# Block-sparse attention and a max-out feed-forward on one core: weights' squares on TensorE, eight places for the weights' loads, queries of four units at once, single-column biases, early sampled copies on GpSimd

## The chip, the core and the metric

One core of one Trainium2 chip. The metric is the device time in microseconds (us) of one execution. Engines are named as in the profile: PE (TensorE; PEld is its weight load), DVE (VectorE), ACT (ScalarE), POOL (GpSimd), SP (SyncE, here a queue of DMA issues).

## What is computed

Four batches (B = 4) of eight heads (H = 8), 768 positions (S), head size 64 (D): attention in which each block of 32 queries sees its neighbours, the first and the last block, and three sampled blocks; the queries of the first and the last block see all keys. The 3072 rows of 512 that come out go through a max-out feed-forward.

```python
scores = q @ k.T / sqrt(64)          # kept where |blk_i - blk_j| <= 1, or either block is 0 or 23,
attn = softmax(scores)               # or blk_j is one of the 3 blocks sampled for blk_i
x = (attn @ v) as [3072, 512]
h = max(x @ w1, x @ w2, x @ w3)      # [512, 768] each
out = h @ w_out                      # [768, 512]
```

## The kernel before

**Numbers in pairs.** Each float32 operand is scaled by a power of two and split into a high and a low half-precision part (ACT writes the high part, DVE the low part, or POOL for some); a product is three matmuls (`PASSES`). The scale comes from a sum of squares: ACT's `Square` with an accumulator, then a one-column matmul against `ones` that adds over the partitions (`total`), then three small DVE operations (`scale_of`).

**Units.** A batch has 24 blocks: one global unit "G" (first and last block, against all keys) and eleven sparse units of two blocks. 48 units U run in the order G, the last pair, then the rest; x = U % 12 is the place in the batch. A sparse unit gathers its keys on chip into `kg` (sampled blocks by three copies per block, one each on DVE, POOL and ACT, L595; the window by DVE, L602) and its values by POOL's indirect DMA (L608). Then per half of the heads an item: scores on PE (L677) into one of two pairs of PSUM banks, row maxima on DVE (L656), the bias (maximum times minus the scale, L658), exponentials on ACT (L686), the probabilities turned: in units under `TURNED` by PE, ACT and DVE (L628 to L631), later by ACT's high part, POOL's low part and a DMA transpose on SP (L635, L636, L639), three places (`NPH`) for the parts. Then values on PE (L701), the division on DVE (L759 to L761), and a turn into `xg` (L768 to L773). Queries are prepared 128 rows at a time (`prep_q`, two units; twice the buffer `qn`).

**Feed-forward.** Every four units make 256 rows, and step F of twelve runs 18 groups of 12 matmuls (six f, three weights, L795): the first weight's result goes to `hf` by ACT (L799), the others by DVE's maximum (L802), then the high part to `ht` by ACT (L805) and the low by POOL (L806); three buffers `hf`. Then 36 matmuls with w_out (L819). `ht` has two buffers, F % 2.

**Weights.** Eight groups g (six of w1, w2, w3 and two of w_out), three tiles each: SP loads them as shifted 16-bit data (L364, L367) into one of four places (three in the key buffer `kt1` of the second batch, one in `xg2`), POOL casts a part into `ob` (L371), DVE joins the two (L375) into the float32 tile `m`, which lies in `ht[g % 2]`. ACT squares the whole group (L386), PE adds, DVE scales, ACT and DVE write the two parts (L398, L406). The groups of w_out are split last, when all scales are known (`relative`, L422 to L429).

**The order** on each engine is fixed before the launch by a planner (`Plan.order`): each operation has an assumed cost, the keys that it reads and writes, and a priority (a unit's number; for weights `WPRI + WSL * g`); a key that is rewritten waits for all its readers. Engines then run their lists in order.

Of the kernel before, what the change touches and what calls it, by code (L numbers as in the profile page):

```python
# [30 lines left out]
NK, NPR, NPH, NPT = 2, 3, 3, 4  # L31
PV, TURNED, POOL_LOW = 0.2, 4, ()
TP, HOLD, WPRI, WSL = 0.45, 3.0, 2.5, 0.25
# [111 lines left out]
def tile_block_sparse_attention_maxout_ffn(ctx, tc, q, k, v, sampled, w1, w2, w3, w_out, out):  # L145
    nc = tc.nc
    B, H, S, D = q.shape
    P = 128
# [37 lines left out]
    qn = sbuf([P, H, D], F32, "qn", 2)  # L186
    qt = sbuf([P, 2, G, P], F16, "qt", 2)
# [11 lines left out]
    ht = sbuf([P, NF, 2, 256], F16, "ht", 2)  # L199
# [110 lines left out]
    def registers(t, name, js, pri):  # L310
        def load():
            for i in js:
                block_of((V, L, A)[t], i, t)
        plan.add(name, 0.56 * len(js), load, r=["samp"], w=[("regs", t, js[0])], pri=pri)
# [24 lines left out]
    def next_stage():  # L339
# [3 lines left out]
    kt1 = kts[1].rearrange("p n t g e s -> p (n t g e s)").bitcast(F32)  # L343
    w_stage = [(kt1[:, 1024 * i : 1024 * i + 1024], [("kt", 1, i), ("kt", 1, 3 + i)]) for i in range(3)]
    w_stage += [(xg[i].rearrange("p g t x -> p (g t x)").bitcast(F32),
                 [(y, i, c0) for y in ("xh", "xl") for c0 in range(0, 256, 64)]) for i in (2,)]

    def decode_w(g, pri):

        c = g % 2  # L350
        m = ht[c].rearrange("p f t x -> p (f t x)").bitcast(F32).rearrange("p (k x) -> p k x", k=3)
        mi = m.bitcast(I32)
        mk = [("ht", c, f) for f in range(NF)]
        for k in range(3):
            st, stk = w_stage[(3 * g + k) % len(w_stage)]
# [36 lines left out]
    def split_w(g, parts, sc, keys, pri):  # L392
        m3, hi, lo, mk = parts
        for k in range(3):
            n = m3.shape[1] // 3
            sl = slice(k * n, (k + 1) * n)
            s, mkk = sc[k % len(sc)], mk[2 * k : 2 * k + 2]
# [7 lines left out]
            else:  # L405
                plan.add("DVE", 0.74, lambda sl=sl, s=s: V.scalar_tensor_tensor(  # L406
# [74 lines left out]
    def turn_k(b, pri):  # L481
        sm, sts, kt = ksm[b % 2], k_sts[b], kts[b % NK]
        for a in range(3):
            src = stage[sts[a]].rearrange("p (e g x) -> p e g x", e=2, g=G)
            for half in range(2):
# [8 lines left out]
                hk, lk = [("kt", b % NK, 3 * t + a) for t in range(2)]  # L494
                plan.add("PE", TP, turn, r=SK(sts[a]) + ["ident", ("k", "s", b)], free=[hk, lk],
# [38 lines left out]
    def prep_q(b, n, pri):  # L534
# [381 lines left out]
```

## Time and profile before

| what | value |
|---|---|
| device time, 3 runs | 694.62 us median (694.61 to 694.68) |
| the profiled execution: its own time, its span | 689.42 us, 687.5 us |
| busy PE, DVE, ACT, POOL | 591.3, 411.8, 392.1, 316.8 us |
| mean granted TensorE clock | 0.916 |

The span is counted from the first instruction to the last; the profiled execution's own time is 1.9 us longer than its span, and 5.2 us under the median of the plain runs. A share of busy time is a mean over stages: here a stage of loading and decoding weights, a long one, and a tail. Idle time of an engine matters only where it holds the end.

### The profile page before, as it was taken

The numbers are of one execution on the slowest core, as the hardware profiler recorded it, in microseconds if no ns is written. First come the engines' busy times: TensorE is split into PE (matmuls) and PEld (weight loads), VectorE is DVE, ScalarE is ACT, GpSimd is POOL, SyncE is SP. The second block draws the span as 40 slices with busy tenths as digits, with TensorE's granted clock in tenths as the row PEclk, the third lists the DMA queues.
The fourth block names the chain that finished last, engine by engine and source line by source line (L and its number), as shares of the span: only waits on it lengthen the run. The fifth ranks groups of instructions, "written<-read, shape, count | busy, mean of one in ns | idle before, by whom it ended". The sixth has DMA issues, their size and how long they took to land.

```text
span 687.5 us, 25107 instructions
## 1 busy us (share of the span) xinstructions
PE 591.3 (86%) x10576; PEld 442.2 (64%) x10576; DVE 411.8 (60%) x1022; ACT 392.1 (57%) x830; POOL 316.8 (46%) x414
## 2 busy tenths in 40 slices
PE   2586468359999979999999789989999789999997
PEld 2354347236885856875876666866776675778684
DVE  1678779983666876498555664676547675422110
ACT  4646667667636766776547656855558556312121
POOL 1354356463534665364554563446455756511110
PEclk9756559559999989999999999999999999999999
DMA  9684788779967799987997889996987979830000
GB/s 212 187 249 131 233 217 202 159 151 221 222 121 169 92 200 211 199 198 165 169 169 138 148 177 174 195 234 132 188 126 148 176 144 174 175 61 25 17 17 32
DMA packets 197044, 109.28 MB, mean 159 GB/s; under 512 B 161073, under 2 KB 182594, under 8 KB 196930
## 3 DMA queue, kind: packets, MB, share of 16 engines
q1 hardware_dynamic: 187074, 72.51, 57.1%
q0 software_dynamic: 9856, 35.15, 20.5%
q8 instruction: 83, 1.36, 0.9%
q14 instruction: 31, 0.25, 0.1%
HBM read 68.72 MB, written 12.70 MB: 118 GB/s over the span
## 4 chain that ended last, share of the span: by engine, by line
PE 70%; DVE 13%; issue 9%; ACT 2%; DMA 2%; POOL 1%; SPq 1%; DVEq 0%; POOLq 0%; ACTq 0%
PE f_ps L795 37%; PE f_ps L819 13%; PE av_ps L701 5%; PE s_ps L677 4%; PE s_ps L720 2%; DVE nm L656 2%; PE tp_ps L559 2%; PE tp_ps L492 1%; DVE nm L658 1%; PE tp_ps L768 1%; PE tp_ps L332 1%; DVE w_hl L406 1%; DVE vhl L520 1%; DVE kg L602 1%; PE av_ps L742 1%
## 5 line engine op out<-in xcount | busy, mean ns | idle before, releaser
L795 PE MATMUL f_ps<-xg,w_hl 128*128 128x256 f16 x2592 | 308.4, 278 | 15.7 <-issue 7.3
L795 PEld LDWEIGHTS <-w_hl 128*128 128x128 f16 x2592 | 254.6, 100 | 58.4 <-issue 23.5
L636 POOL TENSOR_TENSOR phl<-pr,phl 128x512 f16<-128x512 f32 (+1 forms) x106 | 119.1, 1130 | 81.1 <-ACT phl L635 51.8
L802 DVE SCALAR_TENSOR_TENSOR hf<-f_ps,hf 128x256 f32<-128x256 f32 x144 | 60.7, 421 | 114.6 <-PE f_ps L795 103.3
L806 POOL TENSOR_TENSOR ht<-hf,ht 128x256 f16<-128x256 f32 x72 | 50.4, 701 | 147.2 <-ACT ht L805 147.0
L686 ACT ACTIVATE pr<-s_ps,nm,qsm 128x256 f32<-128x256 f32 x176 | 92.2, 564 | 40.7 <-DVE nm L658 27.9
L608 POOL DMA_INDIRECT vg<-vscr,rows_of x88 | 83.6, 950 | 53.4 <-PE av_ps L701 37.2
L819 PE MATMUL f_ps<-wo_hl,ht 128*128 128x512 f16 x432 | 98.7, 380 | 0.0
L656 DVE TENSOR_REDUCE nm<-s_ps 128x2 f32<-128x512 f32 x88 | 60.2, 684 | 24.9 <-PE s_ps L677 18.5
L805 ACT CAST ht<-hf 128x256 f16<-128x256 f32 x72 | 28.9, 403 | 79.0 <-DVE hf L802 78.9
L819 PEld LDWEIGHTS <-ht 128*128 128x128 f16 x432 | 40.8, 98 | 46.9 <-issue 3.1
L635 ACT CAST phl<-pr 128x512 f16<-128x512 f32 (+1 forms) x106 | 61.7, 592 | 5.7 <-DMA pts<-phl 5.3
L595 POOL COPY kg<-kt 128x256 f16 x88 | 37.9, 450 | 53.8 <-PE s_ps L677 41.1
L701 PE MATMUL av_ps<-vg,pts 128*32 128x65 f16 (+1 forms) x4224 | 50.3, 200 | 13.2 <-issue 7.4
L701 PEld LDWEIGHTS <-pts 128*32 128x32 f16 x4224 | 41.5, 98 | 29.0 <-issue 20.9
L677 PE MATMUL s_ps<-kg,qt 64*32 64x256 f16 x2112 | 48.5, 294 | 10.8 <-ACT pr L686 4.4
L658 DVE TENSOR_SCALAR nm<-nm,qsm 128x2 f32<-128x2 f32 (+1 forms) x104 | 46.5, 448 | 2.2
L799 ACT ACTIVATE hf<-f_ps 128x256 f32<-128x256 f32 x72 | 27.5, 382 | 30.8 <-PE f_ps L795 30.3
L595 ACT COPY kg<-kt 128x256 f16 x88 | 32.7, 404 | 16.7 <-PE s_ps L677 13.2
L677 PEld LDWEIGHTS <-qt 64*32 64x32 f16 x2112 | 24.3, 95 | 22.7 <-issue 13.3
L825 ACT ACTIVATE ob<-f_ps,vsm 128x512 f32<-128x512 f32 x24 | 16.5, 686 | 26.9 <-PE f_ps L819 26.8
L595 DVE COPY kg<-kt 128x256 f16 x88 | 30.6, 381 | 1.5 <-issue 1.3
(138 smaller groups left out, 661.2 us busy)
## 6 DMA issues: line engine op xcount, KB each, us to landing
kt<-in_moe_w_dram SPq DMA_DIRECT2D x14, 511.0 KB, 4.1
vscr<-vhl SPq DMA_DIRECT2D x12, 520.0 KB, 4.5
stage<-in_k_dram SPq DMA_DIRECT2D x24, 256.0 KB, 5.6
stage<-in_v_dram SPq DMA_DIRECT2D x12, 512.0 KB, 8.0
qn<-in_q_dram SPq DMA_DIRECT2D x20, 256.0 KB, 5.0
out_dram<-ob SPq DMA_DIRECT2D x20, 256.0 KB, 2.1
vg<-vscr SPq DMA_DIRECT2D x16, 130.0 KB, 3.8
kt<-in_moe_w_out_dram SPq DMA_DIRECT2D x4, 511.8 KB, 4.6
```

What stands on the lines that cost most here:

```text
L595: (A.copy if t == 2 else eng.tensor_copy)(out=dst, in_=src)
L608: plan.add("POOL", 1.02, lambda c=c: L.indirect_dma_start(out=vgj[: 6 * HB, c].rearrange("p e h x -> p (e h x)"), out_offset=None, in_=vsc ...
L635: plan.add("ACT", 0.05 + 0.565 * n / 512, lambda: A.copy(out=hl[:, :n], in_=prt[:, :n]), r=[("pr", it % NPR)], w=[hk], pri=pri)
L636: plan.add("POOL", 1.2 * n / 512, lambda: L.tensor_tensor(out=hl[:, n : 2 * n], in0=prt[:, :n], in1=hl[:, :n], op=ALU.subtract), r=[("pr", ...
L656: plan.add("DVE", 0.7, lambda: V.tensor_reduce(out=n[:, 0:2], in_=both()[:, :, :256], axis=AX.X, op=ALU.max), w=[ks], pri=pri, drop=job)
L658: plan.add("DVE", 0.23, lambda: V.tensor_scalar(out=n[:, 2 : 2 + w], in0=n[:, :w], scalar1=sm[:, 5:6], scalar2=LN_TOP, op0=ALU.mult, op1=A ...
L677: T.matmul(out=s_ps[r * BS : (r + 1) * BS, hd * 512 : hd * 512 + 256], lhsT=q_t[hp, tq, 2 * i + u, q0 + c * BS : q0 + (c + 1) * BS], rhs=k ...
L686: plan.add("ACT", 0.56, lambda hd=hd: A.activation(out=prt[:, hd * 256 : hd * 256 + 256], in_=s_of(job)[:, hd * 512 : hd * 512 + 256], fun ...
L701: T.matmul(out=av_ps[r * BS : (r + 1) * BS, 2 * i + hd, :w], lhsT=pv[:, tp, hd, e, r * BS : (r + 1) * BS], rhs=vgj[:, c, e, h, (D + 2) * t ...
L795: T.matmul(out=pf, lhsT=w_hl[f][:, j, g, wp], rhs=x[:, g, xp, :], start=g == 0 and n == 0, stop=g == G - 1 and n == 2)
L802: plan.add("DVE", 0.42, lambda h=h, pf=pf: V.scalar_tensor_tensor(out=h, in0=pf, scalar=2.0 ** -14, in1=h, op0=ALU.mult, op1=ALU.max), r=[ ...
L819: T.matmul(out=f2_ps, lhsT=hts[:, f, hp, t * P : (t + 1) * P], rhs=wo_hl[f // 3][:, f % 3, wp], start=f == 0 and n == 0, stop=f == NF - 1 ...
```

## The change

- The sum of squares of a weight group: twelve matmuls of each 128 x 128 piece with itself (the upper half of each float32, as bfloat16) add up in one bank, and one DVE operation multiplies that with the identity and sums it. ACT's `Square` goes.
- `m` lies in `kt1` (two halves) and no longer in `ht`; `ht` has one buffer. Loads go to `xg1`, `xg2` and the six `stage` buffers.
- `prep_q` takes 256 rows (four units): one square of 1024 columns, one scale, two turns. `qn` has one buffer of twice the size, and `qt` is twice as wide.
- The bias of an item is two operations of one column, and each exponential waits for its own.
- In units up to 8 the third sampled copy is POOL's, and POOL loads the block numbers for it.
- `NPH` 4, `TURNED` 2, `WPRI` 3.0, `WSL` 0.35, and some assumed costs.

```diff
-NK, NPR, NPH, NPT = 2, 3, 3, 4
-PV, TURNED, POOL_LOW = 0.2, 4, ()
-TP, HOLD, WPRI, WSL = 0.45, 3.0, 2.5, 0.25
+NK, NPR, NPH, NPT = 2, 3, 4, 4
+PV, TURNED, POOL_LOW = 0.2, 2, ()
+TP, HOLD, WPRI, WSL = 0.45, 3.0, 3.0, 0.35
...
-    qn = sbuf([P, H, D], F32, "qn", 2)
-    qt = sbuf([P, 2, G, P], F16, "qt", 2)
+    qn = sbuf([P, 2, H, D], F32, "qn")
+    qt = sbuf([P, 2, G, 2 * P], F16, "qt", 2)
...
-    ht = sbuf([P, NF, 2, 256], F16, "ht", 2)
+    ht = sbuf([P, NF, 2, 256], F16, "ht")
...
+    w_stage = [(xg[i].rearrange("p g t x -> p (g t x)").bitcast(F32), XK(i)) for i in range(1, 3)]
+    w_stage += [(stage[i], SK(i)) for i in range(6)]
...
-        m = ht[c].rearrange("p f t x -> p (f t x)").bitcast(F32).rearrange("p (k x) -> p k x", k=3)
+        m = kt1[:, c]
-        mk = [("ht", c, f) for f in range(NF)]
+        mk = [("wm", 3 * c + k) for k in range(3)]
...
-        plan.add("ACT", 1.5, lambda: A.activation(out=hi, in_=m3, func=AF.Square, accum_out=ss[:, 1:2]),
-                 r=mk, w=[("wss", c)] + [("w", g, k, 0) for k in range(3)], pri=pri)
+        def gram():
+            for k in range(3):
+                for x in range(4):
+                    y = mb[:, k, x * P : (x + 1) * P]
+                    T.matmul(out=bank(tr)[:, :P], lhsT=y, rhs=y, start=k == x == 0, stop=k == 2 and x == 3)
+        plan.add("PE", 0.8, gram, r=mk, pri=pri, mode="t", take=tr)
+        plan.add("DVE", 0.3, lambda: V.scalar_tensor_tensor(
+            out=junk[:, :P], in0=bank(tr)[:, :P], scalar=1.0, in1=ident, op0=ALU.mult, op1=ALU.mult, accum_out=ss[:, 1:2]),
+            r=["ident"], w=[("wss", c)], pri=pri, drop=tr)
...
+        parts = [(0, 0, 3 * BS, S - 3 * BS), (3 * BS, 0, BS, 0)] if n == 0 else [(0, 0, P, r0)]
+        for p0, e, w, r in parts + [(0, 1, P, r0 + P)]:
+            plan.add("SP", 0.7, lambda p0=p0, e=e, w=w, r=r: Y.dma_start(out=qn[p0 : p0 + w, e], in_=src[r : r + w]),
+                     w=[("qn", e, p0 > 0)], pri=pri, land=2.0, move=1.3)
...
+                by = 1 if t == 2 and pri < 8 else t
...
+    for t in range(3):
+        registers(t, 1 if t == 2 and 8 > 4 else t, first if t else first + more, -9 + t / 10)
...
-        plan.add("DVE", 0.23, lambda: V.tensor_scalar(
-            out=n[:, 2 : 2 + w], in0=n[:, :w], scalar1=sm[:, 5:6], scalar2=LN_TOP, op0=ALU.mult, op1=ALU.add),
-            r=[ks, cq], w=[ks], pri=pri)
+        for x in range(w):
+            plan.add("DVE", 0.16, lambda x=x: V.tensor_scalar(
+                out=n[:, 2 + x : 3 + x], in0=n[:, x : x + 1], scalar1=sm[:, 5:6], scalar2=LN_TOP, op0=ALU.mult, op1=ALU.add),
+                r=[ks, cq], w=[(ks, x)], pri=pri)
```

The order on ACT, from the last splits of the weights before, and around the first `ht` of the feed-forward now (`w_hl3` is the fourth group of w1 to w3, `wo_hl` are the two of w_out, the number behind a name's last underscore is the buffer's):

```order
L398 ACTIVATE wo_hl0_69<-ht0_133,w_t_75 128x512 x3
L805 CAST ht0_133<-hf0_130 128x256
L805 CAST ht0_133<-hf1_131 128x256
L805 CAST ht0_133<-hf2_132 128x256
L398 ACTIVATE wo_hl1_70<-ht1_134,w_t_75 128x512
L799 ACTIVATE hf0_130<-f_ps1_145 128x256
L398 ACTIVATE wo_hl1_70<-ht1_134,w_t_75 128x512 x2
```

```order
L822 ACTIVATE hf0_130<-f_ps0_143 128x256
L709 ACTIVATE pr1_113<-s_ps1_141,nm3_111,qsm1_100 128x256
L412 ACTIVATE w_hl3_66<-kt1_90,w_s_72 128x4x128 x3
L657 CAST phl2_117<-pr0_112 128x512
L828 CAST ht_133<-hf0_130 128x256
L709 ACTIVATE pr1_113<-s_ps1_141,nm3_111,qsm1_100 128x256
```

Before, the first three high parts into `ht0` stand behind the first split of w_out, which reads its `m` there; now the first stands behind the fourth of the eight groups.

The order on POOL among the casts for the weights, before and now, in each case from a cast of the weights (L371, now L375):

```order
L371 CAST ob0_135<-kt1_90 128x512
L636 TENSOR_TENSOR phl1_117<-pr1_114,phl1_117 128x512
L636 TENSOR_TENSOR phl2_118<-pr2_115,phl2_118 128x512
L307 TENSOR_LOAD samp_87
L307 ISA x2
L595 ISA
L595 COPY kg0_92<-kt0_89 128x256
L371 CAST ob1_136<-kt1_90 128x512
```

```order
L375 CAST ob0_134<-stage5_83 128x512
L375 CAST ob1_135<-xg2_129 128x512
L307 TENSOR_LOAD samp_87
L307 ISA x2
L616 ISA
L616 COPY kg1_93<-kt0_89 128x256
L307 TENSOR_LOAD samp_87
L307 ISA x2
L616 ISA
L616 COPY kg1_93<-kt0_89 128x256
```

`TENSOR_LOAD` fetches a block number into a register; per unit there are now four copies on POOL with four such loads, where two of each stood, and the loads come from `stage` and `xg2`.

## Rows read from the trace of the kernel before

**Rows 1.** The page: the span in 40 equal slices, busy share in tenths, and the granted clock of PE in tenths.
```profile
PE   2586468359999979999999789989999789999997
DVE  1678779983666876498555664676547675422110
PEclk9756559559999989999999999999999999999999
```

**Rows 2.** Busy time of the engines in three stretches: start and end, length, busy us (instructions) of PE, PEld, DVE, ACT and POOL, the granted clock, the DMA share, GB/s.
```profile
0.00:153.40 153.40, 89.25 (x1566) 63.47 (x1567) 115.49 (x272) 97.42 (x187) 70.98 (x111) 0.67 0.76 194
153.40:220.90 67.50, 66.81 (x1000) 49.05 (x998) 37.37 (x95) 40.58 (x83) 28.80 (x34) 0.98 0.85 180
220.90:687.50 466.60, 435.19 (x8014) 329.70 (x8012) 258.98 (x656) 254.07 (x562) 217.01 (x270) 0.99 0.79 144
```

**Rows 3.** The timeline of PE: start, length, line, operation, tiles, count, and in brackets the idle time before it and what ended it.
```profile
110.93 5.59 PE L795 MATMUL f_ps<-xg,w_hl 128*128 128x256 f16 x48
...
150.92 5.16 PE L795 MATMUL f_ps<-xg,w_hl 128*128 128x256 f16 x24 [4.63 <-ACT hf L799]
156.01 0.56 PE L701 MATMUL av_ps<-vg,pts 128*32 128x65 f16 x48
...
162.62 0.52 PE L677 MATMUL s_ps<-kg,qt 64*32 64x256 f16 x24
...
172.50 1.46 PE L819 MATMUL f_ps<-wo_hl,ht 128*128 128x512 f16 x6
...
210.29 0.44 PE L768 MATMUL tp_ps<-ident,xr 128*128 128x128 f32 x2
...
220.72 4.09 PE L795 MATMUL f_ps<-xg,w_hl 128*128 128x256 f16 x36
```

**Rows 4.** The timelines of ACT and of DVE around 150 us.
```profile
146.99 1.95 ACT L398 ACTIVATE wo_hl<-ht,w_t 128x512 f16<-128x512 f32 x3 [1.84 <-DVE w_t L429]
148.84 1.00 ACT L805 CAST ht<-hf 128x256 f16<-128x256 f32 x3
151.89 1.49 DVE L406 SCALAR_TENSOR_TENSOR wo_hl<-ht,w_t,wo_hl 128x512 f16<-128x512 f32 x2
```

**Rows 5.** Groups of DVE's instructions from 0 to 150 us, by shape: busy us and mean ns of one, then the idle time before them.
```profile
L406 DVE SCALAR_TENSOR_TENSOR w_hl<-ht,w_s,w_hl 128x512 f16<-128x512 f32 x18 | 16.9, 983 | 0.0
L375 DVE SCALAR_TENSOR_TENSOR ht<-kt,ob 128x512 int32<-128x512 int32 x18 | 14.8, 842 | 1.1 <-POOL ob L371 1.0
L656 DVE TENSOR_REDUCE nm<-s_ps 128x2 f32<-128x512 f32 x19 | 12.9, 681 | 0.2 <-PE s_ps L677 0.2
L658 DVE TENSOR_SCALAR nm<-nm,qsm 128x2 f32<-128x2 f32 x19 | 10.2, 535 | 0.3
L602 DVE COPY kg<-kt 128x1536 f16<-128x1536 f16 x11 | 6.0, 549 | 0.0
L595 DVE COPY kg<-kt 128x256 f16 x22 | 5.5, 285 | 1.2 <-issue 1.1
L631 DVE TENSOR_TENSOR pts<-s_ps,pts 128x512 f16<-128x512 f32 x4 | 2.6, 681 | 1.1 <-ACT pts L630 1.1
L802 DVE SCALAR_TENSOR_TENSOR hf<-f_ps,hf 128x256 f32<-128x256 f32 x6 | 2.5, 419 | 3.7 <-PE f_ps L795 3.4 <-ACT pr L686 0.2
L658 DVE TENSOR_SCALAR nm<-nm,qsm 128x1 f32<-128x1 f32 x4 | 0.8, 212 | 0.1
```

**Rows 6.** Four lines of DVE over the whole span: least, median and greatest duration in ns.
```profile
L658 DVE TENSOR_SCALAR nm<-nm,qsm x104: 203/228/3021, 32.5 to 592.2; 128x2 f32<-128x2 f32 x88, 128x1 f32<-128x1 f32 x16
L551 DVE TENSOR_SCALAR qsm<-qsm x24: 153/154/156, 16.0 to 557.1; 128x1 f32<-128x1 f32 x24
L406 DVE SCALAR_TENSOR_TENSOR w_hl<-ht,w_s,w_hl x18: 735/744/3317, 61.3 to 128.3; 128x512 f16<-128x512 f32 x18
L375 DVE SCALAR_TENSOR_TENSOR ht<-kt,ob x18: 675/689/1598, 45.9 to 134.6; 128x512 int32<-128x512 int32 x18
```

**Rows 7.** The timeline of all engines around 120 us.
```profile
119.70 3.02 DVE L658 TENSOR_SCALAR nm<-nm,qsm 128x2 f32<-128x2 f32 x1
120.41 2.27 POOL L636 TENSOR_TENSOR phl<-pr,phl 128x512 f16<-128x512 f32 x2
122.63 0.35 DVE L595 COPY kg<-kt 128x256 f16 x2
122.84 0.56 ACT L686 ACTIVATE pr<-s_ps,nm,qsm 128x256 f32<-128x256 f32 x1 [2.00 <-DVE nm L658]
```

**Rows 8.** Groups of POOL's instructions from 0 to 150 us, as in rows 5.
```profile
L371 POOL CAST ob<-kt 128x512 f16<-128x512 bf16 x18 | 15.0, 835 | 14.9 <-DMA kt<-in_moe_w_dram 12.3 <-DVE ht L375 2.5
L595 POOL COPY kg<-kt 128x256 f16 x22 | 11.7, 541 | 32.1 <-PE s_ps L677 24.8 <-DVE kt L502 6.4 <-issue 0.8
L636 POOL TENSOR_TENSOR phl<-pr,phl 128x512 f16<-128x512 f32 x9 | 11.4, 1269 | 4.7 <-ACT phl L635 4.7
```

**Rows 9.** The start: the timelines of ACT and POOL, and one later row of POOL with the gap that the load of a block number leaves.
```profile
6.90 0.63 ACT L543 ACTIVATE junk<-qn 128x512 bf16<-128x512 f32 x1 [4.67 <-issue]
7.06 0.99 POOL L414 MEMSET ob<- 128x512 int32 x2 [4.79 <-issue]
19.88 0.76 POOL L371 CAST ob<-kt 128x512 f16<-128x512 bf16 x1 [11.82 <-DMA kt<-in_moe_w_dram]
104.25 0.49 POOL L595 COPY kg<-kt 128x256 f16 x1 [0.30 <-issue]
```

More of the change, by code (lines that the diff above doesn't have):

```diff
@@ L308, in block_of, with registers @@
         return regs[eng, i, t]
-    def registers(t, name, js, pri):
+    def registers(t, by, js, pri):
         def load():
             for i in js:
-                block_of((V, L, A)[t], i, t)
-        plan.add(name, 0.56 * len(js), load, r=["samp"], w=[("regs", t, js[0])], pri=pri)
+                block_of((V, L, A)[by], i, t)
+        plan.add(("DVE", "POOL", "ACT")[by], 0.56 * len(js), load, r=["samp"], w=[("regs", t, js[0])], pri=pri)
     def scale_of(p2, s, ss):
@@ L494, in turn_k @@
                 hk, lk = [("kt", b % NK, 3 * t + a) for t in range(2)]
+                more = [("wm", 2 * a + x) for x in range(2)] if b == 1 else []
                 plan.add("PE", TP, turn, r=SK(sts[a]) + ["ident", ("k", "s", b)], free=[hk, lk],
@@ L504, in low @@
                         op0=ALU.mult, op1=ALU.subtract)
-                plan.add("ACT", 0.69, high, w=[hk], pri=pri, drop=job)
-                plan.add("DVE", 0.75, low, r=[hk], w=[lk], pri=pri, drop=job)
+                plan.add("ACT", 0.69, high, w=[hk] + more, pri=pri, drop=job)
+                plan.add("DVE", 0.75, low, r=[hk], w=[lk] + more, pri=pri, drop=job)
     KT = lambda b: [("kt", b % NK, i) for i in range(6)]
@@ L617, in tile_block_sparse_attention_maxout_ffn @@
     it_no = [0]
+    PRK = lambda it: [("pr", it % NPR, h) for h in range(2)]
     def probs(n, it, pri):
@@ L682, in scores @@
                         )
-        plan.add("PE", 0.36, scores, r=[("qh", q_c % 2), ("ql", q_c % 2)] + KG(j), pri=pri, mode="s", take=job, pair=True)
+        plan.add("PE", 0.36, scores, r=QT(q_c) + KG(j), pri=pri, mode="s", take=job, pair=True)
         bias, ks = softmax_bias(it, job, sm, ("cq", q_c % 4), False, pri)
@@ L725, in scores @@
                         )
-        plan.add("PE", 1.2, scores, r=[("qh", q_c % 2), ("ql", q_c % 2)] + KT(b), pri=pri, mode="s", take=job, pair=True)
+        plan.add("PE", 1.2, scores, r=QT(q_c) + KT(b), pri=pri, mode="s", take=job, pair=True)
         bias, ks = softmax_bias(its[0], job, sm, ("cq", q_c % 4), True, pri)
@@ L836, in tile_block_sparse_attention_maxout_ffn @@
     first = [1 + 2 * m + c for m in [order[1]] + order[2:5] for c in range(2)]
-    for t, name in enumerate(("DVE", "POOL", "ACT")):
-        registers(t, name, first if t else first + [1 + 2 * m + c for m in order[5:8] for c in range(2)], -9 + t / 10)
+    more = [1 + 2 * m + c for m in order[5:8] for c in range(2)]
+    for t in range(3):
+        registers(t, 1 if t == 2 and 8 > 4 else t, first if t else first + more, -9 + t / 10)
     prep_k(0, -5.5)
```

103 lines of the change are left out of this document (51 added, 52 removed).

## The prediction

> **What bounds the kernel now.** First the span in slices [rows 1]: PE stands at 7 to 9 tenths or more from about 155 us to the end, and ahead of that DVE is the fullest row, with 7 to 9 tenths between 35 and 155 us, while PE's granted clock is 5 or 6 tenths in most of those slices (the lower of its two levels, 1.2 GHz, around slices in which it was half idle). So there are two kernels: up to about 153 us one bounded by DVE's list, which carries the attention of the first units and the decoding of the weights, and then one bounded by PE. The three stretches say the same [rows 2]: 115.5 of 153.4 us busy on DVE first; then PE 66.8 of 67.5 us; then PE 435.2 of 466.6 us. Work that DVE, ACT or POOL lose after 153 us is therefore worth little by itself; what counts is when PE's full stretch begins, and how much of PE's work has been done by then.
>
> PE's timeline shows where that is decided [rows 3]. Feed-forward step 0 has begun by 111 us, but 48 matmuls (four of its 18 groups) from 110.9 us on are its last for a while: the next 24 start at 150.9 us, behind ACT's `hf`. ACT's timeline gives the reason [rows 4]: the first three high parts into `ht` run at 148.84 us, straight behind the split of w_out that ends there, since the float32 tile of that group lies in `ht0`. The three `hf` buffers are full until then. So step 0 was held by the weights' last split, which its first 18 groups don't need.
>
> **The change, part by part.** The mark that I use is M, the end of DVE's last split of w_out: 153.4 us before [rows 4].
>
> *DVE up to M.* I count both orders up to that split and price by the groups of this stretch [rows 5]. The new order has done less attention by then: 4 row maxima less (4 x 0.681 = 2.7 us), 2 windows and 4 sampled copies less (2 x 0.549 + 4 x 0.285 = 2.2). Four probability blocks of units 2 and 3 are no longer turned by way of DVE (4 x 0.681 = 2.7). Three preparations of queries fall away, five small operations of about 0.154 us each [rows 6] = 2.3. It has done more of the feed-forward: 5 maxima (5 x 0.419 = 2.1) and one division (0.7: two small operations and one as long as a maximum). New are eight sums of a diagonal, 128 x 128: not shown before; the nearest rows are a one-column operation at 0.154 [rows 6] and a 128 x 256 one from PSUM at 0.419 [rows 5], ends of 1.2 and 3.4 us in all. I take 0.32, 2.6 us, nearer the second, which reads PSUM as well.
>
> *The bias.* 19 pairs at 0.535 and 4 single ones at 0.212 cost 11.0 us [rows 5]. The pair's median over the whole span is 0.228 with a maximum of 3.021, while the one-column operation at L551 never leaves 0.153 to 0.156 [rows 6]. At 119.70 us one sees what stretches it [rows 7]: a pair ends at 122.72 us, when POOL's two subtractions end (122.68), and ACT's exponential waits 2.00 us of that. Single columns: 34 x 0.212 = 7.2 us, 3.8 less. But the copies that stand behind the pair read and write the same memories, and may wait for POOL in its place; so I hold half of the stretch (19 x (0.535 - 0.228) = 5.8, half 2.9) as moved, and book 0.9 us. The ends are 5.8 less (34 x 0.154) and 7.2 more (34 x 0.535, if columns are stretched as pairs are). The Trainium skill (VectorE: DVE Perf Modes, Rules for kernel authors) asks for few operations on DVE, not many, which speaks against this edit; by that the split would only add instructions, 15 x 0.212 = 3.2 us at the undisturbed price, and a result of that kind is the fourth rival below.
>
> Together DVE has -2.7 - 2.2 - 2.7 - 2.3 + 2.1 + 0.7 + 2.6 - 0.9 = -5.4 us up to M.
>
> *The start.* The first queries are now three loads ahead of the keys on SP instead of two: 256 KB more, at the 194 GB/s of the first stretch [rows 2] 1.3 us. ACT no longer fetches block numbers (it was held till 6.90 us by them [rows 9]), but squares twice the width, another 0.6 us [rows 9]; one more turn of queries lies beside the keys' turns, for which I take 0.3. In all 2.2 us. On POOL eight more loads of block numbers stand ahead of the zeroing of `ob`, which was done at 8.05 us, and eight took at most 4.8 us [rows 9]; the first cast came at 19.88 us, waiting for its load, so 7 us of cover are left. On SP the second load of queries now waits for PE's turn of the first, since `qn` has one buffer, and the weights' loads are queued behind it. I book nothing: two weights' tiles are loaded ahead of it and eight places cover the rest; without that cover M is later by as much as the loads are.
>
> *POOL.* Up to M it gets 16 copies (16 x 0.541 = 8.7), four subtractions (4 x 1.269 = 5.1) and eight loads of block numbers between its casts (8 x 0.30 = 2.4): 16.2 us on top of 71.0 of 153.4 [rows 2, 8, 9]. That is 57% of the stretch, and it waited 24.8 us for scores ahead of its copies [rows 8], so I take this as covered, except that a fuller POOL stretches DVE's two-source operations more. Their stretch, mean over median, is 18 x (0.983 - 0.744) = 4.3 us in the weights' low parts and 18 x (0.842 - 0.689) = 2.8 in the joins [rows 5, 6]; a quarter more of 7.1 is 1.8 us. Ends: 0 and 16.2.
>
> *ACT* loses eight squares and 16 copies up to M; it was 97.4 of 153.4 us busy [rows 2], less than DVE and behind it, so nothing is booked. *Eight places for loads*: the casts waited for a load of weights 12.3 us, at the start alone [rows 8]: nothing. *Squares on PE*: 12 matmuls of 128 columns, at most what 12 of 256 columns take, 5.59 / 4 = 1.4 us at the high clock and 5.16 / 2 = 2.6 at the low [rows 3], in a stretch where PE was idle for 64 of 153.4 us [rows 2]: nothing, unless their bank is late.
>
> M after the change: 153.4 - 5.4 + 2.2 + 1.8 = 152.0 us.
>
> *What PE has done by M.* This is the main term. Before, step 0 ended at 172.50 + 1.46 = 173.96 us [rows 3]. In the new order all 18 groups of step 0 stand ahead of the last split; what is left is its 36 matmuls with w_out, at 1.46 / 6 = 0.24 us each [rows 3] 8.8 us and two items of scores of 0.52 us, of which some 2 us run while w_out's second half is being split: the end is at 152.0 + 7.5 = 159.5 us, 14.5 earlier. Against that, PE has less attention behind it there: two units of scores (4 x 0.52) and one item of values (0.56), 2.6 us [rows 3]. Lead: 11.9 us.
>
> *What of it lasts.* Steps 0 and 1 are followed by step 2, whose rows come from units 8 to 11. Before, the last of these was turned at 210.29 + 0.44 = 210.7 us and step 2 began at 220.7 us [rows 3]: 10.0 us in hand. If the attention becomes no earlier, a lead of 11.9 loses 1.9. DVE is busy for only 37.4 of 67.5 us in that stretch [rows 2], so it may become earlier; I book 10.0 us. After 220.9 us both orders hold PE alike; half as many preparations of queries, quicker biases and a fourth buffer of parts against 16 loads of block numbers that ACT now does later: nothing.
>
> Sum against the profiled execution: 689.4 - 10.0 = 679.4 us. Its time is 5.2 us under the median of the plain runs, so the median goes from 694.6 to **684.6 us**, 1.4% less. A difference of 0.2% (1.4 us) is about what a measurement of this kernel can tell from none.
>
> **The rivals.**
> 1. *The rest gains too.* PE is idle 31.4 us after 220.9 us [rows 2]. If some of that is attention that arrives late, and if units 8 to 11 come earlier by the whole lead, 8 to 10 us more: 675. For it: the bias lies between scores and exponentials of every item. Against it: PE is the fullest there by far.
> 2. *The lead is given back.* At M the new order is behind by two and a half units of scores, and the keys of the second batch can only be turned when `kt1` is free of weights. If the last unit of the batch is turned 5 us later than before, at 216 us, step 2 starts 4 us earlier and not 10: 690.6.
> 3. *POOL takes DVE's place* (slower). Every group of weights needs three casts, and these stand behind copies that wait for scores of an earlier unit; in units 5 to 8 a unit has four copies with four loads (4 x 0.84), two subtractions (2.5) and some three casts (2.5), over 8 us of POOL beside two gathers [rows 8, 9]. If the whole 16.2 us lie on the chain, M is 152.0 - 1.8 + 16.2 = 166.4 us, step 0 ends at 173.9 as before, and with 2.6 us of attention missing the run takes 697.2. It decides from 13.7 us on the chain (the 11.9 of the lead and the 1.8 that are booked). Against it: the waits of 24.8 us that can be filled [rows 8].
> 4. *The single columns don't help.* The wait moves to the next copies, as the order at 122.63 us suggests [rows 7], and columns are stretched as well: the bias costs 7.2 us more instead of 0.9 less, M is at 160.1 and the lead 3.8: 690.8. The Trainium skill (SBUF — State Buffer, Who interferes with whom) says that a DVE copy or scalar operation in a two-port mode and a POOL instruction exclude each other for the whole of an instruction; the row at 119.70 us agrees, and by that rule the copies behind would wait as the pairs did.
>
> **How the numbers follow.** Forecast 0.42, first rival 0.18, second 0.14, third 0.16, fourth 0.10. Faster by over 0.2%: the forecast, the first, and most of the second and fourth, 0.78. Within 0.2%: the edges of the second, third and fourth, 0.08. Slower: the rest of the third and a little of the second, 0.14. The range runs from the first rival (674) to the third (697), with a later POOL than that left out.
>
> **What would show it.** Right: matmuls of L818 (L795 before) run without a break of 30 us from their first to the end of step 0, which ends near 160 us; the first `ht` stands far ahead of w_out's split; M near 152 us; single columns at 0.15 to 0.21 us with no value over 1 us; step 2 near 210 us; PE idle after that about 31 us. Wrong: casts of weights that are late and wait for nothing but POOL's own list, M beyond 160 us (third rival); PE idle between steps 1 and 2 (second); long copies in place of long biases (fourth); a PE that is idle for less than 25 us after step 2 begins (first).

## The result, and the profile after

The changed kernel takes **701.5 us** (median of four, 700.3 to 702.8), the kernel before 694.7 in the same session: ratio **1.0098** (95% interval 1.0078 to 1.0118), 6.9 us slower. The forecast was 684.6, faster, with a range that ended at 697. It failed in sign and size. Ratios here and below compare, of each kernel, the runs within 1.5% of its fastest.

The profiled execution took 702.0 us, its span is 700.2. It lies 0.5 us over its median and that of the kernel before 5.2 under its own, so the two spans differ by 12.7 us where the medians differ by 6.9: differences read between these two profiles are together some 6 us too large, and where in the run these 6 us lie is not known. First the three stretches, cut at the new M (161.0 us) and at the new beginning of step 2, columns as in [rows 2]:
```profile
0.00:161.00 161.00, 100.33 (x1701) 74.36 (x1702) 113.16 (x279) 78.06 (x144) 83.27 (x132) 0.73 0.82 195
161.00:222.49 61.49, 57.21 (x884) 40.32 (x883) 33.90 (x97) 38.08 (x75) 23.02 (x28) 0.94 0.73 177
222.49:700.20 477.71, 444.67 (x8050) 334.10 (x8048) 240.24 (x687) 260.25 (x557) 220.26 (x274) 0.97 0.76 142
```
M came 7.6 us later, not 1.4 earlier. DVE was busy a little less up to it than before, but idle for longer, and the third stretch is 10.9 us longer than the 466.8 us from 220.72 to the end before [rows 3]. The timeline of PE, against [rows 3]:
```profile
111.53 0.69 PE L791 MATMUL s_ps<-ident,xr 128*128 128x128 f32 x2 [7.95 <-ACT pr L709]
...
115.47 2.54 PE L818 MATMUL f_ps<-xg,w_hl 128*128 128x256 f16 x12
...
166.56 1.47 PE L842 MATMUL f_ps<-wo_hl,ht 128*128 128x512 f16 x6
...
214.92 0.66 PE L575 MATMUL tp_ps<-ident,qn 128*128 128x128 f32 x4 [0.18 <-DVE qt L581]
217.14 0.69 PE L791 MATMUL tp_ps<-ident,xr 128*128 128x128 f32 x2 [1.56 <-DVE qt L581]
217.76 2.13 PE L743 MATMUL s_ps<-kt,qt 64*64 64x384 f16 x12
219.82 0.69 PE L791 MATMUL tp_ps<-ident,xr 128*128 128x128 f32 x2
220.44 2.12 PE L743 MATMUL s_ps<-kt,qt 64*64 64x384 f16 x12
222.49 4.92 PE L818 MATMUL f_ps<-xg,w_hl 128*128 128x256 f16 x24
```
The break of 30 us in step 0 is gone, and step 0 ends at 168.0 us, 6 earlier than before. But step 2 begins 1.8 us later, because the rows of unit 11 are turned at 219.8 us and not at 210.3. PE was half idle ahead of it, and then its granted clock is 0.50, the lower of its two levels (columns as in [rows 2], the clock third from the end):
```profile
212.30:217.00 4.70, 2.58 (x107) 1.83 (x105) 2.99 (x12) 2.06 (x3) 2.56 (x3) 0.96 0.91 204
217.00:222.49 5.49, 5.35 (x28) 2.33 (x29) 2.02 (x5) 1.62 (x4) 0.19 (x1) 0.50 1.13 259
```
12 global scores take 2.13 us there instead of the 1.16 that they take at the high level.

What comes after step 2 begins, after and before (PE's groups: busy us and mean ns of one):
```profile
L818 PE MATMUL f_ps<-xg,w_hl 128*128 128x256 f16 x2160 | 257.5, 279 | 2.9 <-issue 2.0 <-DVE hf L825 0.8
L743 PE MATMUL s_ps<-kt,qt 64*64 64x384 f16 x122 | 11.3, 330 | 0.0
```
```profile
L795 PE MATMUL f_ps<-xg,w_hl 128*128 128x256 f16 x2160 | 253.6, 276 | 11.0 <-issue 7.3 <-DVE hf L802 3.7
L720 PE MATMUL s_ps<-kt,qt 64*64 64x384 f16 x96 | 8.5, 326 | 0.0
```
PE's busy time there is 9.3 us more, its idle time (33.0 us) only some 2: 2.8 us are global scores and 3.3 sparse scores, part of which had been done by then before, and 3.9 are the same feed-forward matmuls at a lower clock on average (0.97 instead of 0.99). The time is lost between steps 3 and 4, which begin 61.2 us apart in the change (282.8 and 344.0 us) and 46.3 apart before (278.4 and 324.7): the rows of units 18 and 19 stand in PE's list behind turns of the third batch's keys (L506), each of which waits for DVE's low part of the one before, and when step 3 is done, at 330.8 us, PE has little else. The clock falls there too. PE's rows and two stretches of the change, then a row and a stretch of the kernel before:
```profile
333.04 0.66 PE L506 MATMUL tp_ps<-ident,stage 128*128 128x128 f32 x4 [1.22 <-DVE kt L517]
340.16 0.69 PE L791 MATMUL tp_ps<-ident,xr 128*128 128x128 f32 x2 [1.56 <-DVE kt L517]
```
```profile
332.00:338.00 6.00, 3.08 (x107) 2.52 (x108) 3.89 (x10) 4.04 (x8) 1.72 (x2) 0.84 1.02 253
338.00:344.00 6.00, 2.45 (x9) 1.20 (x8) 3.99 (x15) 2.75 (x7) 2.76 (x6) 0.50 1.10 213
```
```profile
319.41 0.38 PE L768 MATMUL tp_ps<-ident,xr 128*128 128x128 f32 x2
```
```profile
318.00:324.00 6.00, 5.28 (x73) 2.69 (x71) 5.50 (x15) 5.27 (x12) 2.84 (x5) 1.00 0.45 112
```

**The start.** SP, ACT and PE of the changed kernel (start, length, engine, line, idle before):
```profile
23.16 2.70 SPq L556 DMA_DIRECT2D qn<-in_q_dram  x2
25.97 5.23 SPq L368 DMA_DIRECT2D stage<-in_moe_w_dram  x3
32.21 1.06 ACT L559 ACTIVATE junk<-qn 128x1024 bf16<-128x1024 f32 x1 [5.22 <-DMA qn<-in_q_dram]
33.41 0.58 PE L332 MATMUL s_ps<-qsm,ones 128*128 128x1 f32 x2 [3.97 <-ACT junk L559]
34.25 1.97 PE L575 MATMUL s_ps<-ident,qn 128*128 128x128 f32 x8 [0.25 <-DVE qsm L319]
36.15 1.17 PE L743 MATMUL s_ps<-kt,qt 64*64 64x384 f16 x6
```
and the first scores before:
```profile
29.38 2.13 PE L720 MATMUL s_ps<-kt,qt 64*64 64x384 f16 x12
```
The second block of queries is loaded from 23.2 us on, when PE has turned the first, and lands at 32.2 us beside three loads of weights. In PE's list its sum of squares and its turn stand ahead of the first global scores, which need neither: these come 6.8 us later than before.

**DVE and POOL.** DVE's groups up to M, against [rows 5], and two lines with least, median and greatest duration in ns, against [rows 6]:
```profile
L420 DVE SCALAR_TENSOR_TENSOR w_hl<-kt,w_s,w_hl 128x512 f16<-128x512 f32 x18 | 16.7, 956 | 0.0
L379 DVE SCALAR_TENSOR_TENSOR kt<-stage,ob 128x512 int32<-128x512 int32 x19 | 14.3, 759 | 1.5 <-POOL ob L375 1.5
L616 DVE COPY kg<-kt 128x256 f16 x18 | 11.1, 644 | 1.4 <-issue 1.4
L623 DVE COPY kg<-kt 128x1536 f16<-128x1536 f16 x9 | 6.5, 718 | 0.0
L681 DVE TENSOR_SCALAR nm<-nm,qsm 128x1 f32<-128x1 f32 x34 | 6.1, 207 | 0.4
```
```profile
L681 DVE TENSOR_SCALAR nm<-nm,qsm x192: 198/205/216, 39.3 to 598.2; 128x1 f32<-128x1 f32 x192
L616 DVE COPY kg<-kt x18: 214/224/3658, 45.6 to 146.7; 128x256 f16 x18
```
Single columns are never stretched (198 to 216 ns). What the pairs lost, the copies behind them lose now: 18 x (644 - 224 ns) = 7.6 us in single blocks, where it was 22 x (285 - 220) = 1.4. The longest copy, DVE and POOL around it:
```profile
81.26 1.63 POOL L616 COPY kg<-kt 128x256 f16 x3
82.22 3.79 DVE L616 COPY kg<-kt 128x256 f16 x2
82.86 1.15 POOL L658 TENSOR_TENSOR phl<-pr,phl 128x512 f16<-128x512 f32 x1
83.96 0.75 POOL L375 CAST ob<-stage 128x512 f16<-128x512 bf16 x1
84.64 1.15 POOL L658 TENSOR_TENSOR phl<-pr,phl 128x512 f16<-128x512 f32 x1
85.93 0.41 DVE L796 TENSOR_TENSOR xg<-s_ps,xg 128x256 f16<-128x256 f32 x1
```
The second of DVE's two copies took 3.658 us. It ends at 86.01 us, 0.22 us (the median of such a copy) after POOL ran out of work at 85.79, behind a copy, a subtraction, a cast and a subtraction. The Trainium skill (SBUF — State Buffer, Who interferes with whom) has one instruction wait for the whole of the other; the row shows a wait over several in a row.

The waits up to M (engine, what waited, for what: us, times, longest), of ACT, PE and POOL:
```profile
ACT pr L709 <- DVE nm L681: 14.9, 6, 3.2
```
```profile
PE s_ps L791 <- ACT pr L709: 17.2, 3, 8.0
```
```profile
POOL ob L375 <- DVE kt L379: 26.3, 6, 12.5
```
The first two form a chain: an exponential waits for its bias, and PE's next turn waits for the bank of scores that the exponential reads. POOL is only a part of what makes the bias late. PE's wait of 5.42 us that ends at 95.99 us goes back to these rows:
```profile
89.42 0.68 DVE L678 TENSOR_REDUCE nm<-s_ps 128x2 f32<-128x512 f32 x1
90.02 2.29 DVE L420 SCALAR_TENSOR_TENSOR w_hl<-kt,w_s,w_hl 128x512 f16<-128x512 f32 x3
92.22 0.88 DVE L379 SCALAR_TENSOR_TENSOR kt<-xg,ob 128x512 int32<-128x512 int32 x1
93.03 0.32 DVE L681 TENSOR_SCALAR nm<-nm,qsm 128x1 f32<-128x1 f32 x2
```
The maxima are done, and their bias stands behind three low parts and a join of weights, which take some 0.3 us more than at the medians of [rows 6]: there the place in DVE's list costs, and not POOL. The longest wait, to 111.53 us, goes back to both: one bias stands behind low parts and joins again, the other behind a join that waited 1.26 us for POOL's cast. Nor do the casts' waits close a ring: 22.1 of the 26.3 us are two waits that end at 52.9 and 73.8 us, ahead of the copy that was held.

### The profile page after: what moved, and what is told of

Its sections match the earlier page's. It is cut to its first block, busy times and chain, and to the rows that moved or that the text cites. A ratio compares the mean times of both kernels' runs of the same rounds, so it can differ in the third digit from the quotient of the medians.

```text
span 700.2 us, 25389 instructions
## 1 busy us (share of the span) xinstructions
PE 602.2 (86%) x10632; PEld 448.8 (64%) x10632; DVE 387.3 (55%) x1062; ACT 376.4 (54%) x774; POOL 326.5 (47%) x434
## 4 chain that ended last, share of the span: by engine, by line
PE 72%; issue 6%; DVE 6%; DMA 5%; ACT 3%; POOL 3%; SPq 1%; POOLq 1%; another core or an unknown queue 0%; DVEq 0%; ACTq 0%
PE f_ps L818 38%; PE f_ps L842 13%; PE s_ps L700 5%; PE av_ps L724 4%; PE s_ps L743 3%; DMA pts<-phl 3%; PE tp_ps L791 2%; PE tp_ps L506 1%; PE av_ps L765 1%; DMA qn<-in_q_dram 1%; PE tp_ps L575 1%; ACT pr L709 1%; PE tp_ps L332 1%; POOL phl L658 1%; DMA xg<-in_moe_w_dram 1%
## 5 line engine op out<-in xcount | busy, mean ns | idle before, releaser
L658 POOL TENSOR_TENSOR phl<-pr,phl 128x512 f16<-128x512 f32 (+1 forms) x110 | 123.4, 1126 | 98.4 <-ACT phl L657 57.8
L657 ACT CAST phl<-pr 128x512 f16<-128x512 f32 (+1 forms) x110 | 65.4, 594 | 6.8 <-DMA pts<-phl 5.1
L700 PE MATMUL s_ps<-kg,qt 64*32 64x256 f16 x2112 | 51.9, 289 | 17.9 <-issue 10.8
L616 POOL COPY kg<-kt 128x256 f16 x104 | 47.0, 476 | 26.1 <-PE s_ps L700 17.8
L700 PEld LDWEIGHTS <-qt 64*32 64x32 f16 x2112 | 26.3, 94 | 32.2 <-issue 27.3
L616 ACT COPY kg<-kt 128x256 f16 x72 | 27.1, 403 | 28.0 <-PE s_ps L700 18.1
L616 DVE COPY kg<-kt 128x256 f16 x88 | 33.5, 412 | 3.6 <-issue 3.4
L681 DVE TENSOR_SCALAR nm<-nm,qsm 128x1 f32<-128x1 f32 x192 | 32.9, 207 | 2.4
L795 ACT CAST xg<-tp_ps 128x256 f16<-128x256 f32 x44 | 16.3, 370 | 30.5 <-PE tp_ps L791 29.8
```

The source lines that it names most:

```text
L616: (A.copy if by == 2 else eng.tensor_copy)(out=dst, in_=src)
L657: plan.add("ACT", 0.05 + 0.565 * n / 512, lambda: A.copy(out=hl[:, :n], in_=prt[:, :n]), r=PRK(it), w=[hk], pri=pri)
L658: plan.add("POOL", 1.2 * n / 512, lambda: L.tensor_tensor(out=hl[:, n : 2 * n], in0=prt[:, :n], in1=hl[:, :n], op=ALU.subtract), r=PRK(it) ...
L700: T.matmul(out=s_ps[r * BS : (r + 1) * BS, hd * 512 : hd * 512 + 256], lhsT=q_t[hp, tq, 2 * i + u, q0 + c * BS : q0 + (c + 1) * BS], rhs=k ...
```

## The experiments

Ratios are to the kernel before on the same chip, with 95% intervals: runs of one kernel there lie some 1% apart, so a ratio tells more than a median. Times inside a run come from its one profiled execution.

**One edit undone at a time.** Queries for two units again; the second block behind unit 0; the third copies on ACT; the bias in pairs.
```diff
-    qn = sbuf([P, 2, H, D], F32, "qn")          # e1: prep_q and its calls as before
+    qn = sbuf([P, H, D], F32, "qn", 2)
-            r=keys, w=[("qss", c % 4)], pri=pri)                                     # e2
+            r=keys + ([("unit", 0)] if c == 1 else []), w=[("qss", c % 4)], pri=pri)
-                by = 1 if t == 2 and pri < 8 else t                                  # e3, registers too
+                by = t
-        for x in range(w): plan.add("DVE", 0.16, ...)                                # e4
+        plan.add("DVE", 0.23, ... out=n[:, 2 : 2 + w], in0=n[:, :w] ...)
```


> The changed kernel with queries prepared for two units at once, in two qn, as before; all else of the change stays. Theory Q (the run of 701.5 us is late because the second block of queries, whose one qn is free only after PE's turn of the first, stands on PE ahead of the first global scores): these start near 29.4 us instead of 36.2, the last turn of unit 11 comes near 213 us instead of 219.8, and the run takes 688 to 694 us. Theory P (POOL's 16 more copies hold the weights and the first units): scores start earlier but the first matmul of the feed-forward stays at 113 to 116 us, and the run takes 699 to 702. Theory B (single columns of the bias cost more than pairs): no change beyond 1.5 us.

Measured 1.0126 (1.0033 to 1.0219). The first scores came at 35.05 us: here the third block of queries takes the place of the second ahead of them. Theory Q was not tested by this run.

> The changed kernel with one dependence more in the plan: ACT's square of the second block of queries, and so PE's turn of it, is put behind unit 0. Four units at once and one qn stay. Theory Q in its narrow form (only the place on PE matters): first global scores near 30 us, run 693 to 697. Theory Q in its wide form (blocks of four units arrive late everywhere, batch after batch): first scores near 30, run 698 to 702. Theory P: 699 to 702.

Measured 1.0107 (1.0036 to 1.0177). First scores at 29.62 us, unit 0 turned at 57.5 instead of 71.8, step 0 ends at 158.2. Unit 11 is turned at 216.5, step 2 begins at 219.2, and the time is that of the changed kernel: by itself the start is not what the run waits for.

> The changed kernel with the third sampled copies of units 1 to 7 and their block numbers on ACT again, as before. Theory P: POOL's busy time between 60 and 120 us falls from 38.7 us by some 5, the feed-forward's first matmul comes 5 us or more earlier than 115.5, and the run takes 692 to 697. Theory Q: ACT has room for them there (27.7 of 60 us busy), the run stays at 700 to 703.

Measured **0.9981** (0.9926 to 1.0035), some 8 us less than the changed kernel, as theory P had it in sign. Not in its way: POOL's busy time from 60 to 120 us stayed at 38.6 us. M came at 148.1 us, step 0 ended at 156.2, unit 11 was turned at 206.9 and step 2 began at 209.6. Waits of ACT and of PE up to M:
```profile
ACT pr L709 <- DVE nm L681: 5.3, 5, 1.9
```
```profile
PE s_ps L700 <- ACT pr L709: 5.9, 3, 3.1
PE s_ps L791 <- ACT pr L709: 4.8, 2, 4.4
```
Exponentials wait 5.3 us for the bias instead of 14.9. PE waits 4.8 us for them at L791 instead of 17.2, but 5.9 at L700, where it was 0.2. POOL's casts still wait 20.1 us for joins.

> The changed kernel with the bias of both halves by one operation of 128 x 2, as before. Theory B: single columns cost, run 697 to 700. Forecast's own view (columns save): 702 to 706. Theories Q and P: within 1.5 us of 701.5.

Measured 1.0195 (1.0077 to 1.0312), in the direction of the forecast; the interval is too wide to part it from the change.

**The change again, two edits undone, and two parts alone.** The second run has the edits of e2 and e3 together. The others take the kernel before and add only the copies on POOL, or only the weights (`decode_w`, places, one `ht`, kt1's keys).

> The changed kernel itself, unaltered, timed beside the kernel before and the runs sent with it. All theories: 699 to 703 us, ratio to the kernel before near 1.010; with that its unit 12 is turned near 220 us and its copies of one block on DVE (median 0.224 us) have values over 3 us again.

Measured 1.0126 (1.0045 to 1.0208), with a copy of 3.652 us at the same place: the result and the row repeat. The places in the run repeat less well: M is 158.2 instead of 161.0, and step 2 begins at 216.9 us, 3.8 us *earlier* than in the kernel before. What this execution loses (it ran 3.2 us over its kernel's median) lies behind that point.

> The changed kernel with both: the third sampled copies on ACT, and the second block of queries behind unit 0. Theory P (POOL's copies cost some 10 us, through DVE's operations that they and POOL's subtractions hold up) and Q in its narrow form (the start, some 3 us at unit 12) together: unit 0 turned near 57 us, unit 12 near 200, run 684 to 690 us. If the two overlap, so that only the later of them counts: 689 to 693.

Measured 0.9876 (0.9780 to 0.9971), from two of its six runs.

> The version with third copies on ACT and the second block of queries behind unit 0 once more, beside the two others: ratio 0.982 to 0.994 to the kernel before if it is faster than both kernels; 0.996 or more would say that its first runs were lucky.

Measured **0.9932** (0.9897 to 0.9966). With third copies on ACT and the second block of queries behind unit 0 the kernel is faster than both. In the second of these runs the first scores are at 29.4 us, M at 148.2, step 0 ends at 156.4, unit 11 is turned at 209.2 and step 2 begins at 211.9, close to the forecast's 210.7.

> The kernel before with one part of the change alone: the third sampled copies of units 1 to 7, and their block numbers, on POOL. Theory P: the copies cost by themselves, since POOL's and DVE's operations then start together when a buffer comes free; M later than 153.4 by 6 us or more, run 698 to 704 us. Rival (POOL had 24.8 us of waits to fill there, and it is the new order of the weights that makes POOL late): 693 to 696.

Measured 0.9997 (0.9948 to 1.0046): theory P falls in its simple form. Sixteen copies on POOL cost nothing that shows in the old order.

> The kernel before with the weights' part of the change alone: decoding in kt1, one ht, eight places for loads, squares by products on PE with a sum of the diagonal on DVE. The forecast's main term: no break of 30 us in step 0, step 0 ends near 160 us instead of 174, step 2 begins near 211 instead of 220.7, run 683 to 688 us. Rival (the lead doesn't last, since units 8 to 11 come no earlier): 692 to 695.

Measured **1.0321** (1.0222 to 1.0421). Step 0 ends at 159.8 us, as the forecast's main term says, and the run is 3% slower: unit 11 is turned at 223.7 us and step 2 begins at 226.8. Here too a block of queries (the third) held PE ahead of the first scores, until 35.3 us.

**What fills POOL, and what the weights need.**
```diff
-PV, TURNED, POOL_LOW = 0.2, 2, ()              # e9, on the changed kernel
+PV, TURNED, POOL_LOW = 0.2, 4, ()
-            r=keys, w=[("qss", c % 4)], pri=pri)                                     # e10, on e8
+            r=keys + ([("unit", 0)] if c == 2 else []), w=[("qss", c % 4)], pri=pri)
-TP, HOLD, WPRI, WSL = 0.45, 3.0, 3.0, 0.35     # e11, on e6
+TP, HOLD, WPRI, WSL = 0.45, 3.0, 3.6, 0.4
```


> The changed kernel with TURNED 4 again: the four probability blocks of units 2 and 3 are turned on PE and copied by ACT and DVE, as before, and POOL is spared four subtractions (4 x 1.2 us) while it keeps the 16 copies. Why did the copies cost some 8 us in the changed kernel and nothing in the kernel before? Theory F (POOL was filled by copies and subtractions together, and DVE's copies are held while subtractions run): run 691 to 696 us, and no copy of one block on DVE over 2 us. Theory O (the order of the new weights, not POOL's load): 698 to 703, as the changed kernel.

Measured 1.0023 (0.9985 to 1.0062), 5 us less than the change; up to M the longest copy of a block is 1.099 us (2.947 later), PE's wait at L791 for exponentials 1.2 us instead of 17.2. By the ratios copies and subtractions together are what costs: either taken off POOL gives most of it back. The trace doesn't show the way: M is 158.4 and step 2 begins at 217.4 us, no earlier than in the repeat of the change (e5).

> The kernel before with the weights' part alone, as in the run of 709 us, and with the third block of queries put behind unit 0, since there its square held PE ahead of the first global scores until 33.8 us (9.7 us from issue to landing beside three loads of weights). Theory Q: unit 0 is turned near 57 us instead of 67.6, unit 11 near 212 instead of 223.7, run 688 to 696 us. Theory A (the new order of the weights by itself sets the attention back): first scores near 29.5 us, but unit 11 at 219 or later and a run over 700.

Measured 1.0105 (1.0046 to 1.0165). About two thirds of the loss were the start; but unit 11 is turned at 221.6 us, so theory A holds for the rest: the weights' new order by itself sets the attention back.

> The fastest version so far (third copies on ACT, second block of queries behind unit 0; ratio 0.988 to the kernel before) with the weights later: WPRI 3.6 and WSL 0.40 instead of 3.0 and 0.35. There PE ended step 1 at 195.7 us and step 2 began at 208.7, so attention, not the feed-forward, was late. If attention gains what the weights lose: M near 152 us, step 0 ends near 160, unit 11 turned near 200 and the run 0.5 to 1% faster than that version. If the weights then hold step 0: no gain, ratio 0.988 to 0.998.

Measured 1.0049 (1.0009 to 1.0089). Later weights moved M to 157.4 and unit 11 to 213.2, both later: no gain.

> The fastest version so far with the bias of both halves by one operation of 128 x 2. Theory of the forecast (columns save part of the pair's stretch, 0.9 us booked, up to 5.8): ratio to the kernel before 0.988 to 0.996. Fourth rival (columns only move the wait to the copies behind them, 15 operations more): 0.980 to 0.987.

e4's edit on e6. Measured 1.0043 (1.0002 to 1.0084), 1.1% over its twin. ACT's wait for the bias, in pairs and (e15) in columns:
```profile
ACT pr L708 <- DVE nm L680: 12.0, 7, 4.6
```
```profile
ACT pr L709 <- DVE nm L681: 6.4, 4, 2.6
```
In the new order columns are worth more than was booked.

**Where the lead is given back, and how the parts add.**
```diff
-            prep_q(nx // 12, nx % 12 // 4, nx - 2.0)                                 # e13, on e6
+            prep_q(nx // 12, nx % 12 // 4, nx - (2.0 if U < 9 else 0.5))
```


> The version with third copies on ACT and the second block of queries behind unit 0 (ratio 0.988), and with the later blocks of queries (from unit 9 on) half a unit ahead of their use in the plan instead of two. In that version PE was without work from 195.6 to 208.7 us: the two turns of the next queries (198.5 and 200.7 us) stood in the one bank ahead of the rows of units 10 and 11 (203.4 and 206.0), for which step 2 waited. Theory T (the double turn ahead of the rows is what gives the lead back at each batch): unit 11 turned near 200 us, step 2 begins near 204, ratio 0.978 to 0.985. Rival (rows wait for attention itself, and the later queries then delay the next units): step 2 near 208, ratio 0.986 to 0.995.

Measured 1.0038 (0.9993 to 1.0083). The edit moved the queries' turns behind unit 10 but not behind unit 11, and the run became slower. Theory T is not borne out; what holds units 9 to 11 stays open.

> The changed kernel with the third copies on ACT and queries for two units at once as before, their third block put behind unit 0. It differs from the version of ratio 0.988 in the queries alone. Theory Q wide (blocks of four units cost at each batch): ratio 0.975 to 0.985. Forecast's view (half as many preparations, nothing or a little gained by four): 0.987 to 0.998.

e1 and e3 together, with e10's edit. Measured 0.9874 (0.9821 to 0.9926), no other than the four-unit version within the intervals: blocks of four give nothing that shows.

The three last have the bias in columns on the kernel before (e16) and on e10 (e17), and the change's `NPH`, `TURNED`, `WPRI`, `WSL` on e10 (e18); with both on e10, and two costs that the planner assumes for copies, one has e14.

> The kernel before with one part of the change alone: the bias by single columns. The forecast booked 0.9 us for it: ratio 0.997 to 1.000. Fourth rival (the wait moves to the copies): 1.000 to 1.004. Theory C, after the run in which the pair cost 1.1% in the new order (columns shorten the way from scores to exponentials in every unit, before and after w_out's split): 0.985 to 0.995.

Measured 0.9997 (0.9962 to 1.0031): the fourth rival, or the booked 0.9 us, but not theory C. The copies of this kernel up to M:
```profile
L595 DVE COPY kg<-kt 128x256 f16 x22 | 10.9, 505 | 2.8 <-issue 2.4
```
They took 285 ns each with pairs [rows 5]. So 22 x 220 ns = 4.8 us of what the pairs lost moved into them. One of these copies, at 95.2 us, is held for 4.301 us, longer than any in the change; the exponential behind it waits 2.98 us for its bias, and the run is no slower for it.

> The weights' part with the third block of queries behind unit 0 (ratio 1.0105), and single columns as well. Theory C: 0.995 to 1.002. If columns are worth their booked 0.1% alone: 1.007 to 1.013.

Measured 1.0024 (0.9992 to 1.0056), at the edge of theory C.

> The weights' part with the third block of queries behind unit 0 (ratio 1.0105), and the change's numbers for the order: four buffers of parts, probabilities of units 2 and 3 by POOL and DMA (TURNED 2), weights later (WPRI 3.0, WSL 0.35); the bias stays in pairs. Theory W (weights that are decoded early set the attention back, so later ones give back part of 1 to 3%): 0.993 to 1.002, unit 11 turned at 214 us or earlier instead of 221.6. Rival (these numbers do nothing by themselves): 1.006 to 1.014.

Measured 1.0144 (1.0086 to 1.0202): the numbers alone do nothing for the better. Unit 11 is turned at 213.7 us and step 2 begins at 216.8, 3.9 us earlier than before, as theory W had it, and still the run is 1.4% slower. Yet columns and numbers together (e14) go from 1.0105 to 0.9874, while each alone gives 0.8% and nothing. The parts don't add: the planner lays out every list anew, so no edit here changes one thing alone.

## Why the prediction was wrong, step by step

Times in us, one profiled execution each; the two columns on the right are other kernels than the change.

| | before | forecast | change | change again (e5) | e3 | e15 |
|---|---|---|---|---|---|---|
| first global scores | 29.4 | 31.6 | 36.2 | 36.0 | 35.8 | 29.4 |
| M | 153.4 | 152.0 | 161.0 | 158.2 | 148.1 | 148.2 |
| step 0 ends | 174.0 | 159.5 | 168.0 | 163.5 | 156.2 | 156.4 |
| unit 11 turned | 210.3 | | 219.8 | 214.2 | 206.9 | 209.2 |
| step 2 begins | 220.7 | 210.7 | 222.5 | 216.9 | 209.6 | 211.9 |
| from there to the end | 466.8 | 466.8 | 477.7 | 480.0 | 472.1 | 472.4 |

Forecast and result are 0.9856 and 1.0098 of the kernel before, 2.4% or 17 us apart. Undoing POOL's copies gives back 1.2% (e3), putting the second block of queries later 0.5% more (e15), and 0.8% are left in e15, where step 2 begins nearly as forecast; by the intervals each of these shares is uncertain by about half a per cent.

- **POOL: the step that failed most.** "I take this as covered": 1.8 us were booked with 16.2 as the other end. With the third copies back on ACT the run is 1.2% faster, some 8 us, and M 12.9 us earlier (10.1 against e5). The cover was counted in POOL's idle time (24.8 us of waits), and e7 shows that in the old order there is room for 16 copies. That the edit costs in the new order is shown; the way is not. The rows suggest that DVE had no room: copies, subtractions and casts of POOL one after another hold a copy for 3.66 us, and bias, exponential, bank and PE follow late. But a wait of PE of 5.42 us goes back to DVE's own work on the weights, in e16 a longer hold cost nothing, and e9 has no such hold up to M and the same M as e5.
- **The start: mis-sized.** 2.2 us were booked, 6.8 measured. The sentence "I book nothing" looked at the weights' loads behind the waiting load, and not at who waits for that load: PE, whose list has the second block's turn ahead of the first scores. Alone it costs nothing at the end (e2); once POOL is relieved the ratio goes from 0.998 to 0.988 and 0.993 with it (e6, e15), but the intervals overlap. Only under the weights' new order alone is its price clear of noise, some 2% (e8 to e10).
- **DVE's list up to M** was right in kind. The sums of a diagonal took 0.286 + 0.083 us where 0.32 was taken; single columns 0.207 as forecast. Nearly all of the stretch moved to the copies behind (4.8 of 5.8 us in e16), not half of it as booked. With POOL relieved M is 148.1, below the forecast's 152.0, though the start is late.
- **What PE has done by M: right.** No break in step 0, which ends 7.0 us after M (7.5 forecast, though its terms add up to 7.8). *Squares on PE* took 0.85 to 1.5 us a group (1.4 to 2.6 had been the most), and *eight places* put three loads of weights beside the queries' load in the start; a price of their own was not measured for either.
- **What of it lasts: wrong in the change, nearly right in e3 and e15**, where step 2 begins within 1.2 us of the forecast.
- **"After 220.9 us: nothing": wrong in all.** From step 2 to the end the 17 profiled executions with the weights' new order took 472.1 us or more, the three with the old order (before, e7, e16) 470.5 or less. So a lead at step 2 is given back behind it: e5 and e18 begin it 3.8 and 3.9 us earlier than before and are 1.3 and 1.4% slower. The 10.9 us of the change are too many, since one kernel's executions differ here by 2 to 4 us (e5; e6 and e15) and the profiled execution before is 5.2 us under its median: by the medians 6.9 - 1.8 = 5.1 us, an estimate. The place is the same in all: from the beginning of step 3 to that of step 4 it is 50.2 us or more under the new order (61.2 in the change, 60.3 in e5) and 48.6 or less under the old. A feed-forward that is ahead of its attention runs out of rows there, and PE idles into the low clock. Whether the next batch's keys are to blame was not tested: no run puts them elsewhere. I had subtracted missing attention at M and did not count again at step 2. The weights alone (e8, e10) show another way: step 0 ends up to 20 us earlier, unit 11 is turned 11 to 13 later, and the run is 1 to 3% slower.

Of the rivals, the first falls: PE is idle for 33.0 us after step 2 begins. The third had the engine and nearly the time (697.2, M 166.4), but not the way: casts waited 26.3 us for DVE's joins, not for POOL's own list. The second was seen too, with unit 11 at 219.8 instead of its 216. The fourth is right that the wait moves to the copies, wrong that columns are stretched (216 ns at most), and right about the kernel before (e16); in the new order columns are worth some 1% (e12).

By which way POOL's copies cost 8 us, why units 9 to 11 come late under the new weights, and why numbers and columns help only together, was not settled.

## What to carry to other kernels

Idle time of an engine covers only its own list: before work is moved onto it, look at which operations of its neighbours run at the same moments, and who waits for those in a chain; then undo the move by itself, since a long wait in a trace need not be what costs. Where a moved preparation lands in an in-order list, ask what stands behind it, with the load's real time to landing. And a consumer that is ahead keeps its lead only if its next input comes earlier too.

## What the runs showed of the hardware

A DVE copy of 128 x 256 (median 0.224 us) took 3.658 us beside POOL, 3.652 when repeated and 4.301 in e16, while the one-column operations of the bias never left 0.198 to 0.216 us in the change; pairs had gone up to 3.021 [rows 6]. Two loads of queries of 256 KB took 9 us from the first issue to the wait's end, beside three loads of weights.
